# A new seed list for the list-scheduled order of a window-attention and mixer kernel

## The chip, the cores and the metric

The kernel runs on one core of one Trainium2 chip. The metric is device time in microseconds (us) from launch to end. The kernel before takes 262.97 us, the median of three runs (262.75 to 263.44). One further execution was recorded by the hardware profiler. Its span from the first to the last instruction is 261.5 us, and every time below that is not called a run time is taken from that record.

## The reference

Attention with four sink tokens and a window of 128 runs on (batch, heads, sequence, head size) = (4, 8, 768, 64). Its output, with the heads side by side as 512 columns, goes through a mixing layer along the sequence and a two-layer perceptron along the channels. All inputs and the output are float32.

```python
scores = q @ k.T / 8                       # per batch and head
keep   = (column < 4) | (0 <= row - column < 128)
a      = softmax(where(keep, scores, -1e9))
x      = a @ v                             # (4, 768, 512) with the heads side by side
a1     = alpha1 * x + beta1
u      = x + lam * (w_tok @ a1)            # w_tok is 768 x 768, over the sequence
a2     = alpha2 * u + beta2
out    = u + lam * (relu(a2 @ w_ch1) @ w_ch2)   # 512 -> 2048 -> 512
```

## The kernel before

The kernel does not issue its work in a written order. It first makes a list of tasks. A task is a short run of instructions on one engine (for example four matmuls, or one evacuation), with a priority, the engines that may do it and an expected duration on each in ns, the tasks that it needs, and the buffers that it uses.

```python
def add(self, prio, engs, fn, after=(), uses=(), mode=None, lands=None, port=False, since=0.0):
    t = Task(len(self.tasks), prio, engs, fn, after, uses, mode, lands, port, since)
```

A planner on the host then walks through time. Among the open tasks it takes the one that can start first by the expected durations; the rank, that is the order of the priorities, breaks ties. If a task has several engines it goes to the one where it would end first. The planner also gives out the buffers, so an order decides engines and buffers too. Two things are charged on TensorE: 95 ns whenever the packing of the array changes (`mode`), and a wait. Up to 36 us of planned time it fills waits of TensorE with matmuls on a constant tile ("idle" matmuls, whose result nobody reads).

```python
key = (at_e + FW * t.engs[e], at_e, r, at_e + t.engs[e], i, e)
# ... (cut: the choice of the best key over the open tasks)
n = int((start - max(free[PE], 400.0)) / (took if free[PE] > 4500.0 else 110.0))
if e == PE and free[PE] < until and n > 0:
    # ... (cut: takes a spare accumulator, if there is one)
    idle = (min(spare)[1], n)
# ... (cut)
if e == PE:
    if start < 4500.0:
        cost = cost * 2
    if t.mode != mode:
        cost = cost + 95
    mode = t.mode
free[e] = start + cost
if e == POOL or (e == DVE and t.port):
    port = free[e]
```

The last lines keep marked VectorE work and all GpSimd work from overlapping in the plan. Transfers go through a model of two queues (those that SyncE issues, those that GpSimd issues) that take turns.

The priorities are written by hand: loads at about -1000, the first attention batch below that or near -900, and the main work of batch b at 100*b and up. Then a list of seeds is applied, one after another. Each seed adds Gaussian noise to a random part of the priorities in one range.

```python
def shuffle(prio, seed):
    rnd = random.Random(seed)
    if seed < 100000:
        lo, hi, wide = -2200.0, 8.0, 10.0 ** rnd.uniform(0.7, 2.7)
    else:
        lo = rnd.choice((0.0, 0.0, 0.0, 50.0, 100.0, 200.0))
        hi, wide = lo + 60.0, 10.0 ** rnd.uniform(0.3, 1.3)
    share = 10.0 ** rnd.uniform(-2.5, -1.0)
    return [p + rnd.gauss(0.0, wide) if lo <= p < hi and rnd.random() < share else p for p in prio]

def emit(self, turns):
    prio = [t.prio for t in self.tasks]
    for seed in turns:
        prio = shuffle(prio, seed)
    for t, e, start, stop, idle in self.run(prio):
        # ... (cut: the instructions of the task are issued on engine e)
```

The tasks that the text speaks of are these. `mlp1` is the first matrix of the perceptron and its evacuation, `mlp2` the second, `tok` the mixing along the sequence, and `cast_w2` folds lam into the second matrix.

```python
# mlp1: four 128x384 matmuls, then relu on ScalarE or VectorE
a = add(p, {PE: 4 * 161}, mm, [...uT, w1...], [ph, bu])
done["h", b, chk, fi] = add(p + 0.1, {ACT: 493, DVE: 556}, relu, [a], [ph, bh])
# mlp2: four 128x512 matmuls of an accumulation over sixteen; the residual is added at its end
a = add(p, {PE: 4 * 214}, mm, [...hT, w2...], [pc, bh])
# tok: six 128x512 matmuls
a = add(p, {PE: 215 * len(sis)}, mm(sis), after, [pt] + [hs[si] for si in sis])
# cast_w2: sixteen of these
add(p, {DVE: 700, POOL: 1270},
    lambda e: engine[e].tensor_mul(w2f[:, a, :], src.t[:, a % 2, :], lam_b), [...wst, lam...], [src], port=True)
# scores of one block of 128 keys: row-packed, two accumulators of their own ("S", two in all)
a = add(p, {PE: cost}, mm, qk + [done["bias"]], [o] + [u[3] for u in units] + more, mode="row")
```

All other TensorE results share four accumulators (`"d": 4`). Per later batch there are six score tasks (row-packed) and one sink task (column-packed).

Of the kernel before, what the change touches and what calls it, by code (L numbers as in the profile page):

```python
# [276 lines left out]
def kernel(  # L277
# [130 lines left out]

    PAIRS = 3

    TURNS = (13523, 134113, 50022, 128275, 136711, 187603, 125671, 100730, 14946, 163131, 178432, 158827, 183776, 137680, 153375, 26742)
    W1_SINCE = 20000.0

    V0 = (((0, 1), (2, 3), (4, 5)), ((0, 1, 2), (3, 4, 5)))
# [799 lines left out]

    plan.emit(TURNS)

# [34 lines left out]
```

The softmax here doesn't subtract the row's maximum and nothing guards it: scores larger than these inputs give would overflow.

## Time and profile before

| | before |
|---|---|
| run time, median of 3 | 262.97 us |
| span in the profile | 261.5 us |
| TensorE matmul, busy | 254.1 us (97%) |
| VectorE, ScalarE, GpSimd, busy | 158.0, 132.5, 78.2 us |
| idle matmuls, busy | 9.5 us, 106 of them |
| mean granted TensorE clock | 1.000 |

The page of a profile has a row of busy times per engine, a strip of 40 slices of the span with the busy share in tenths, the chain of work that ended last (followed back from the last instruction), and the costliest groups of instructions. In a group, the name before the arrow is what is written and the names after it are what is read; then come sizes, type and count, the busy time and the mean of one. PE is TensorE's matmul side, PEld its weight loads, DVE VectorE, ACT ScalarE, POOL GpSimd and SP SyncE, which issues most transfers. The trace can also be asked for a timeline of one engine, for a table of busy times by stretch, and for the waits, that is who kept whom idle. A line such as L1007 is a line of the kernel's file: L1007 is mlp1's matmul, L1013 and L1015 its evacuation on ScalarE and VectorE, L1063 and L1034 mlp2's matmuls, L927 tok, L713 the scores, L909 the folding of lam into the second matrix, L344 the idle matmuls.

### The profile page before, as it was taken

The page shows a single profiled execution, that of the slowest core. Times are in us where ns is not written, and L with a number is a line of the kernel's source. Part 1 is how long each engine was busy: PE and PEld are TensorE (multiplying, and loading weights), DVE is VectorE, ACT ScalarE, POOL GpSimd, SP SyncE. Part 2 cuts the span into 40 slices and gives each one's busy share as a digit, 9 for nine tenths or more (in the row PEclk, how much of TensorE's full clock was granted, in tenths as well). Part 3 has the DMA queues.
Part 4 walks back from the last instruction along what each step waited for, and adds up shares of the span by engine and source line. Part 5 has one row for each costly group of instructions (what it writes and reads, how often), then busy time and mean ns, then how long its engine had stood idle before and what let it go on. Part 6 is the DMA issues. An engine that isn't in the chain of part 4 may idle for free.

```text
span 261.5 us, 4992 instructions
## 1 busy us (share of the span) xinstructions
PE 254.1 (97%) x1974; PEld 141.5 (54%) x1974; DVE 158.0 (60%) x321; ACT 132.5 (51%) x219; POOL 78.2 (30%) x97
## 2 busy tenths in 40 slices
PE   7999998998999999999999999999999999999994
PEld 7755645664555545655555445556554445664452
DVE  5787988989989946268967434376695352000221
ACT  1699746766665123788930133788610226772000
POOL 7429703634652420244544024003123000000000
PEclk9999999999999999999999999999999999999999
DMA  7999999999706987999928989200012136000222
GB/s 208 197 225 327 205 294 387 386 294 240 125 3 172 227 136 181 200 224 224 172 68 135 212 210 211 53 0 3 0 43 81 40 120 83 0 0 3 81 80 80
DMA packets 85839, 38.76 MB, mean 148 GB/s; under 512 B 73508, under 2 KB 79916, under 8 KB 85816
## 3 DMA queue, kind: packets, MB, share of 16 engines
q1 hardware_dynamic: 82032, 35.14, 55.0%
q0 software_dynamic: 3744, 3.28, 7.9%
q8 instruction: 15, 0.25, 0.4%
q14 instruction: 8, 0.07, 0.1%
q10 hardware_dynamic: 40, 0.03, 0.0%
HBM read 29.91 MB, written 6.29 MB: 138 GB/s over the span
## 4 chain that ended last, share of the span: by engine, by line
PE 82%; DVE 6%; DMA 6%; POOL 3%; issue 1%; ACT 1%; SPq 0%; POOLq 0%
PE ch L1063 31%; PE h L1007 28%; PE tok L927 9%; DVE w2f L909 4%; DMA w1f<-in_moe_w_ch_dram 4%; PE pv L803 4%; PE S L713 3%; DMA wst_w<-in_moe_w_ch_dram 2%; PE ch L1034 1%; POOL n L491 1%; PE tp L608 1%; PE tp L605 1%; PE idle L344 1%; DVE hT L1015 1%; ACT uT L951 1%
## 5 line engine op out<-in xcount | busy, mean ns | idle before, releaser
L1007 PE MATMUL h<-uT,w1f 128*128 128x384 f16 x512 | 88.8, 326 | 2.2 <-DVE hT L1015 1.1
L1063 PE MATMUL ch<-w2f,hT 128*128 128x512 f16 x368 | 86.5, 379 | 0.0
L1007 PEld LDWEIGHTS <-w1f 128*128 128x128 f16 x512 | 48.6, 98 | 34.8 <-issue 4.3
L1013 ACT ACTIVATE hT<-h 128x384 f16<-128x384 f32 x100 | 48.8, 490 | 29.5 <-PE h L1007 28.9
L1063 PEld LDWEIGHTS <-hT 128*128 128x128 f16 x368 | 34.3, 98 | 38.0 <-issue 1.1
L845 POOL TENSOR_TENSOR xh<-x,la_b 128x512 f16<-128x512 f32 x18 | 24.3, 1353 | 57.6 <-DVE x L829 57.5
L733 ACT ACTIVATE E<-S 128x1024 f16<-128x1024 f32 (+1 forms) x39 | 37.5, 1001 | 7.3 <-PE S L713 4.7
L1074 DVE TENSOR_TENSOR x<-x,ch 128x512 f32<-128x512 f32 x23 | 15.8, 686 | 35.1 <-PE ch L1063 35.0
L927 PE MATMUL tok<-xh,wtokT 128*128 128x512 f16 x144 | 33.9, 379 | 0.0
L351 ACT CAST u<-x 128x512 f16<-128x512 f32 x18 | 11.1, 618 | 43.1 <-DVE x L934 43.0
L934 DVE TENSOR_TENSOR x<-x,tok 128x512 f32<-128x512 f32 x24 | 16.3, 685 | 19.3 <-PE tok L927 19.3
L927 PEld LDWEIGHTS <-wtokT 128*128 128x128 f16 x144 | 14.0, 98 | 16.5
L852 DVE SCALAR_TENSOR_TENSOR x<-lb_b,rsum,x 128x512 f32<-128x512 f32 x24 | 19.9, 849 | 2.8 <-POOL xh L845 2.6
L829 DVE TENSOR_TENSOR x<-pv,rec 128x256 f32<-128x256 f32 x48 | 20.4, 424 | 1.9 <-DVE rec L828 0.2
L1015 DVE TENSOR_SCALAR hT<-h 128x384 f16<-128x384 f32 x28 | 15.3, 553 | 7.7 <-PE h L1007 7.5
L742 DVE TENSOR_TENSOR E<-E,maskn 128x1024 f16<-128x1024 f16 x24 | 18.4, 795 | 1.8 <-ACT E L733 1.7
L353 POOL CAST vfs<-vnat 128x512 f16<-128x512 f32 x18 | 13.0, 729 | 17.4 <-DMA vnat<-in_v_dram 16.3
L803 PEld LDWEIGHTS <-E 128*128 128x128 f16 x328 | 14.4, 97 | 6.5 <-issue 2.4
L803 PE MATMUL pv<-vfs,E 128*128 128x65 f16 x328 | 17.3, 194 | 0.0
L353 POOL CAST n<-nat 128x768 f16<-128x768 f32 x14 | 12.6, 915 | 14.7 <-DMA nat<-in_k_dram 11.6
L353 POOL CAST u<-x 128x512 f16<-128x512 f32 x6 | 3.7, 621 | 37.8 <-DVE x L934 15.8
L953 DVE TENSOR_SCALAR uT<-uT,ab 128x384 f16<-128x384 f16 x18 | 6.4, 407 | 12.6 <-DMA uT<-u 12.6
(107 smaller groups left out, 218.0 us busy)
## 6 DMA issues: line engine op xcount, KB each, us to landing
out_dram<-x SPq DMA_DIRECT2D x23, 256.0 KB, 2.3
nat<-in_q_dram SPq DMA_DIRECT2D x13, 384.0 KB, 5.8
nat<-in_k_dram SPq DMA_DIRECT2D x13, 384.0 KB, 5.8
vnat<-in_v_dram SPq DMA_DIRECT2D x18, 256.0 KB, 4.6
wst_w<-in_moe_w_ch_dram SPq DMA_DIRECT2D x8, 512.0 KB, 7.3
wtn<-in_moe_w_tok_dram SPq DMA_DIRECT2D x6, 384.0 KB, 4.4
w1f<-in_moe_w_ch_dram POOLq DMA_DIRECT2D x4, 512.0 KB, 10.1
v<-in_v_dram SPq DMA_DIRECT2D x12, 128.0 KB, 5.9
```

The source lines that it names most:

```text
L353: engine[e].tensor_copy(o, i)
L733: nc.scalar.activation(eT.t, pS.t[:, :, 0 : n * w].rearrange("p e (i w) -> p e i w", i=n), AF.Exp, scale=scale)
L742: nc.vector.tensor_mul(ev, ev, m.to_broadcast(list(ev.shape)))
L803: nc.tensor.matmul(po.t[:, hl, :], eT.t[:, e_, off + i, c : c + P], vf[j][:, h, :], start=(r < 2 and n == 0), stop=(n == len(parts) - 1 an ...
L829: nc.vector.tensor_mul(bx.t[:, 4 * G : 4 * G + 4, :], po.t[:, :, 0:D], rec.t.to_broadcast([P, 4, D]))
L845: engine[e].tensor_mul(bh.t, bx.t.rearrange("p h d -> p (h d)"), la1_b)
L852: engine[e].scalar_tensor_tensor(out=xf, in0=lb1_b, scalar=rsum[:, r : r + 1], in1=xf, op0=ALU.mult, op1=ALU.add)
L927: nc.tensor.matmul(pt.t, wtokT[:, si, ti * P : (ti + 1) * P], hs[si].t, start=(si == 0), stop=(si == NR - 1))
L1007: nc.tensor.matmul(ph.t, w1f[:, c, fi * P : (fi + 1) * P], bu.t[:, c, chk * NTOK : (chk + 1) * NTOK], start=(c == 0), stop=(c == NC - 1))
L1013: nc.scalar.activation(bh.t[:, fi, :], ph.t, AF.Relu)
L1015: nc.vector.tensor_scalar_max(bh.t[:, fi, :], ph.t, 0.0)
L1063: nc.tensor.matmul(pc.t, bh.t[:, fi, nt * P : (nt + 1) * P], w2f[:, fi, :], start=(fi == 0), stop=(fi == NF - 1))
```

## The change

Only the list of seeds is replaced: 16 seeds become 51. No instruction is added or removed by hand, and no size, buffer count or expected duration changes. The old list was the outcome of a search that tries seeds and keeps those that help the plan. The new list comes from a longer search over the whole program that may also keep a seed that lengthens the plan a little, so that it can leave a local optimum. The purpose is a better order. The planner reacts to the order with its choices of engine, of buffer and of the number of idle matmuls, so those may change too.

```diff
-    TURNS = (13523, 134113, 50022, 128275, 136711, 187603, 125671, 100730, 14946, 163131, 178432, 158827, 183776, 137680, 153375, 26742)
+    TURNS = (58916, 51094, 164988, 65830, 186405, 183280, 192278, 160001, 176913, 175892, 164653, 178892, 188107, 153507, 192130, 172908, 99824, 189726, 150232, 137815, 195819, 82470, 194072, 21991, 151693, 153696, 416, 91697, 101099, 129663, 169112, 142158, 173756, 141985, 173754, 121021, 159256, 87578, 8213, 167097, 92448, 86502, 130268, 29559, 103092, 138910, 127973, 143653, 120452, 45327, 124786)
```

## The prediction

> **What bounds the kernel now.** I read the busy times first, then the table by stretch, because an average over the span hides where an engine is idle. The busy row of the page:
>
> ```profile
> PE 254.1 (97%) x1974; PEld 141.5 (54%) x1974; DVE 158.0 (60%) x321; ACT 132.5 (51%) x219; POOL 78.2 (30%) x97
> ```
>
> TensorE is the bound; no other engine is busy for over 60%. But 97% counts the idle matmuls as work, and what a new order can win is only what TensorE does not have to do. The table by stretch (length, busy time of each engine with its instructions, clock, DMA share, GB/s) tells where that lies:
>
> ```profile
> 0.00:8.00 8.00, 6.66 (x74) 6.28 (x75) 4.49 (x20) 1.45 (x2) 6.30 (x17) 1.00 0.81 200
> 8.00:30.00 22.00, 21.89 (x323) 13.11 (x320) 18.05 (x50) 20.66 (x33) 12.91 (x21) 1.00 1.16 247
> 30.00:36.00 6.00, 6.00 (x36) 2.94 (x34) 5.93 (x11) 2.05 (x4) 1.11 (x2) 1.00 1.25 209
> 36.00:65.00 29.00, 26.67 (x215) 16.50 (x214) 25.76 (x36) 20.22 (x37) 12.27 (x13) 1.00 1.05 334
> 65.00:250.00 185.00, 185.00 (x1286) 97.73 (x1285) 100.84 (x202) 88.08 (x145) 45.58 (x46) 1.00 0.50 107
> ```
>
> From 65 to 250 us TensorE is busy for 185.00 of 185.00 us. An order can win there only by changing fewer packings, not by filling holes. From 36 to 65 us it is idle for 29.00 - 26.67 = 2.33 us, and VectorE is busy for 25.76 of those 29 us: that is the one stage where another engine holds TensorE up. From 0 to 30 us it looks full, but the same table for the idle matmuls alone says how much of it is filler:
>
> ```profile
> 5.20:8.00 2.80, 2.01 (x28) 1.00 1.12 203
> 8.00:18.00 10.00, 3.17 (x39) 1.00 1.25 215
> 18.00:30.00 12.00, 0.39 (x4) 1.00 1.08 274
> ```
>
> So 39 + 4 = 43 fillers run after 8 us. None run after 30 us.
>
> The timeline of TensorE around the holes (start, duration, group, idle time before it and who ended it):
>
> ```profile
> 39.43 0.32 PE L1007 MATMUL h<-uT,w1f 128*128 128x384 f16 x1 [0.48 <-ACT uT L951]
> 39.94 0.71 PE L1007 MATMUL h<-uT,w1f 128*128 128x384 f16 x2 [0.19 <-DVE uT L953]
> 41.03 2.27 PE L1007 MATMUL h<-uT,w1f 128*128 128x384 f16 x13 [0.38 <-ACT uT L951]
> ...
> 63.15 2.11 PE L1007 MATMUL h<-uT,w1f 128*128 128x384 f16 x12 [1.05 <-DVE hT L1015]
> ```
>
> Three holes at 39 to 41 us wait for the affine evacuations that make the first perceptron input. The largest, 1.05 us, waits for a relu on VectorE. The chain of waits, cut to that place, names what that relu stood behind:
>
> ```profile
> 57.58 0.56 DVE hT L1015
> 58.13 3.48 DVE w2f L909 x3
> 61.61 1.01 DVE E L742
> 62.63 0.48 DVE hT L1015
> 63.11 0.04 issue
> 63.15 2.11 PE h L1007 x12
> ```
>
> Three foldings of the second matrix and one mask, 4.5 us of VectorE, were issued between two relus. Reordering can address exactly this.
>
> **What the Trainium skill says, and whether the trace agrees.** "TensorE: Matmul & The Clock Gate", section "Wait — 56ns, not 53.3ns?", gives the spacing of warm matmuls as N/2.4 GHz + 2.5 ns. For N = 384 that is 162.5 ns; the chain has four mlp1 matmuls in 0.65 us, 162.5 each, so the steady state runs at the spacing of its columns and holds no hidden stall. For N = 128 it is 56 ns; the chain has twelve fillers in 0.67 us, which is 56 each. The section "What's actually happening" of the same page says that TensorE's clock falls to half after an idle window of about 3.4 us. The longest hole after 8 us here is 1.05 us and the granted clock is 1.00 in every stretch: it agrees, and an order would have to open a far longer hole to lose the clock. "SBUF — State Buffer", section "Who interferes with whom", says that a VectorE instruction with two SBUF inputs contends with a GpSimd instruction that reads SBUF. The foldings are such: on VectorE their median is 683 ns and their longest 1752 ns, and GpSimd was casting beside the slow ones. It agrees with that, and means that an order's value depends also on what GpSimd does at that moment.
>
> **The change part by part.** Nothing is removed or added but fillers; the necessary matmuls, evacuations and bytes stay. What moves, I worked out from the seeds: a seed under 100000 disturbs the front (priorities -2200 to 8), any other one of the windows. Evaluating each seed's range and share by the shuffle's own formulas and summing the shares: front 14 seeds and 0.27 expected nudges per task (before 4 and 0.15); window at 0, 6 and 0.28 (3 and 0.18); at 50, 3 and 0.04 (0 and 0); at 100, 7 and 0.28 (3 and 0.09); at 200, 21 and 0.83 (6 and 0.31). So the new list works most on the third batch, where the trace has no hole. Many of those seeds must be walking without gain, as a search that tolerates small losses does.
>
> The terms, each with its upper limit:
>
> 1. **Fillers after 8 us.** 43 x 56 ns = 2.4 us. They lie on the path: each is time in which TensorE had no task ready. They go only if the first attention's loads, casts and exponentials come earlier, and ScalarE is busy for 20.66 of 22 us in that stretch. I expect a fifth: -0.5 us.
> 2. **Holes from 36 to 65 us.** 2.3 us, of which the holes shown make 0.48 + 0.19 + 0.38 + 1.05 = 2.1. The 1.05 us hole needs only another order of VectorE's queue. The others depend on the evacuations after tok. I expect two fifths: -0.9 us.
> 3. **Packing changes.** A row-packed score task of eight 256-column matmuls takes 0.54 us in the chain. Two heads run side by side, so its columns need 4 x (256/2.4 + 2.5) = 0.44 us, and 0.10 us is the change. I counted 70 changes in the matmul records, 40 of them after 50 us, where three batches with seven packed tasks each can have 42 at most. Two S accumulators hold one score task, so two can hardly stand together. Limit about 0.3 us, expected -0.1.
> 4. **The first 8 us and the tail.** The last matmul ends at 257.9 us of 261.5; the residual and the last transfer make the other 3.6 us. The smallest last task is already a half tile, and no seed window reaches the last batch's priorities above 260 (its perceptron stands at 300 and up). Expected 0.
> 5. **Loss against the plan.** The plan counts fixed durations, while the chip showed a folding between 675 and 1752 ns and transfers share one set of queues. A new order fitted to the plan loses a little of its gain: +0.4 us.
>
> Sum: -0.5 - 0.9 - 0.1 + 0.4 = -1.1 us, and 263.0 - 1.1 = 261.9 us. The limits of terms 1 to 3 add to 2.4 + 2.3 + 0.3 = 5.0 us, and 2% is 5.3 us.
>
> **The rivals.** *A wait that takes the place of the one removed.* VectorE's work in 36 to 65 us is 25.76 of 29 us. If the foldings leave the relus' way, they must be done later, before mlp2 first reads them (69.5 us in the timeline), or on GpSimd at 1275 ns and more, where they can block VectorE in turn. For it: VectorE is nearly full. Against it: GpSimd is busy for only 12.27 us there. Result: 262.5 to 263.5 us, no change. *The loads move and the front gets longer.* 14 seeds disturb the front, which holds the order of the first transfers, and the DMA share there is over 1 in three stretches. The first quarter of the first perceptron matrix takes 10.1 us from issue to landing, and its landing at 32.8 us releases the transfers of the second matrix in the chain. For it: the plan's model of two rings is the roughest part. Against it: the old order was found with the same model and filled TensorE well. Result: 264 to 267 us. *A real improvement of the front.* A longer search may have removed most fillers and holes, half to two thirds of 5.0 us: 259.6 to 260.5 us. For it: a search that may go downhill reaches orders that the old one could not. Against it: the 16 old seeds have already taken the cheap gains.
>
> **Range and chances.** I give the middle case (261 to 263.2) six tenths, the improved front two tenths, the longer front somewhat under two tenths. That makes a range of 260.1 to 264.0. Faster by over 2% needs a time under 257.7, which is beyond all three limits together: 0.03. Slower by over 2% needs over 268.2, a stall of 5 us that the old order does not have: 0.03.
>
> **What would show each step.** Term 1: fewer than 43 fillers after 8 us. Term 2: less than 2.3 us idle from 36 to 65 us, with the relu no longer behind three foldings. Term 3: packing changes near 70. Term 4: 3.6 us from the last matmul to the end. The stretch from 65 us on should stay without a hole. The prediction is wrong if the start of the unbroken stretch moves by more than about 2 us, if a hole opens after 65 us, or if ScalarE's first exponentials shift with the loads.

## The result, and the profile after

The changed kernel takes 266.61 us, the median of four runs (266.18 to 268.01). The kernel before, on the same chip, takes 262.94 us. The ratio is 1.0146 (95% interval 1.0104 to 1.0187): slower by about 3.7 us, and outside the predicted range of 260.1 to 264.0 us. The span grew by as much, from 261.5 to 265.2 us. The busy row of the page of the changed kernel:

```profile
PE 255.6 (96%) x1971; PEld 141.5 (53%) x1971; DVE 159.7 (60%) x313; ACT 130.1 (49%) x221; POOL 84.8 (32%) x103
```

TensorE's work is nearly what it was, so the loss is idle time. What grew is GpSimd, from 78.2 to 84.8 us with six instructions more. Among its groups the casts of q and k rose from 14 to 17, and ScalarE's fell from 10 to 7. The table by stretch of the changed kernel (length, busy time and count of TensorE, its weight loads, VectorE, ScalarE and GpSimd, then clock, DMA share, GB/s):

```profile
0.00:8.00 8.00, 6.87 (x82) 6.70 (x82) 3.74 (x18) 2.67 (x3) 7.14 (x20) 1.00 0.74 163
8.00:30.00 22.00, 20.65 (x286) 11.81 (x286) 16.13 (x43) 18.11 (x32) 12.21 (x18) 1.00 1.08 246
30.00:36.00 6.00, 5.52 (x47) 3.00 (x47) 5.85 (x14) 2.16 (x4) 2.91 (x5) 1.00 1.24 207
36.00:65.00 29.00, 28.20 (x220) 16.88 (x219) 26.15 (x34) 18.65 (x38) 14.16 (x15) 1.00 1.04 325
65.00:250.00 185.00, 182.67 (x1274) 96.47 (x1271) 104.98 (x203) 88.47 (x149) 48.37 (x48) 1.00 0.49 110
```

From 36 to 65 us the idle time fell from 2.33 to 0.80 us, as the search meant it to. But 185.00 - 182.67 = 2.33 us of idle time opened after 65 us, where there had been none, and 1.35 + 0.48 us from 8 to 36 us, where there had been 0.11. The same table for the idle matmuls alone:

```profile
5.20:8.00 2.80, 2.21 (x33) 1.00 1.03 147
8.00:18.00 10.00, 2.20 (x21) 1.00 1.11 192
18.00:30.00 12.00, 1.18 (x12) 1.00 1.05 290
```

So 33 fillers ran after 8 us instead of 43. That looks like progress, but only because idle time that no filler covers stands in their place. The timeline of TensorE in the changed kernel shows where the idle time lies and who ended it:

```profile
9.07 0.53 PE L605 MATMUL tp<-iden,n 128*64 128x128 f16 x12 [1.14 <-DMA n<-in_k_dram]
...
66.61 2.76 PE L1007 MATMUL h<-uT,w1f 128*128 128x384 f16 x16 [1.54 <-DVE hT L1015]
...
82.72 0.39 PE L803 MATMUL pv<-vfs,E 128*128 128x65 f16 x7 [0.53 <-DVE E L742]
```

The largest hole, 1.54 us before 66.61 us, is of the same kind as the 1.05 us hole before it, and larger: a relu on VectorE behind foldings and a mask. The chain of waits of the changed kernel, cut to that place:

```profile
59.79 0.96 DVE qkT L353
60.75 4.33 DVE w2f L909 x4
65.08 1.01 DVE E L742
66.09 0.48 DVE hT L1015
66.57 0.04 issue
66.61 2.76 PE h L1007 x16
```

Four foldings take 4.33 us here. In the kernel's own plan the same four stand at 57.26 to 60.06 us and take 2.8 us. The same mask and the same relu follow them there too, but TensorE then waits only 0.04 us.

**Plan against chip.** The planner is part of the kernel, so its planned times can be set beside the record. For the end of the last matmul, with the two seed lists of this case and three orders from the experiments, each from one recorded execution:

| order | seeds | planned | on the chip | lag |
|---|---|---|---|---|
| hand-written priorities only | 0 | 258.11 us | 260.90 us | 2.8 us |
| before | 16 | 254.16 us | 257.90 us | 3.7 us |
| after | 51 | 253.37 us | 261.66 us | 8.3 us |
| mended plan, searched on from the old list | 35 | 254.80 us | 257.37 us | 2.6 us |
| mended plan, searched from the hand priorities | 66 | 254.86 us | 259.48 us | 4.6 us |

The longer search won 0.79 us in its plan and lost 3.76 us on the chip. The question for the experiments is what in the plan did not hold.

**Where the loss arises.** Orders differ, so equal times are not equal progress. I compare the time at which each kernel has done the same amount of necessary matmul work: its columns at the spacing that the prediction used, fillers left out, two heads side by side counted once. The table gives that time minus the time of the kernel before, in us, each from one profiled execution; the last column is the end of the last matmul.

| kernel, and what it is | at 24.1 | 30.5 | 45.5 | 61.1 | 67.7 | 88.3 | end |
|---|---|---|---|---|---|---|---|
| after | +1.28 | +2.13 | +1.54 | +1.67 | +1.88 | +3.47 | +3.76 |
| e5: old front, new rest | +0.82 | +1.18 | +0.24 | +0.09 | +0.28 | +1.86 | +2.15 |
| e6: new front, old rest | +0.76 | +2.44 | +2.46 | +2.14 | +1.96 | +1.97 | +1.97 |
| e7: after, late GpSimd casts on ScalarE | +1.04 | +1.89 | +0.62 | +0.41 | -0.98 | -0.13 | +0.38 |
| e11: e5 and e7 together | +0.95 | +1.30 | +0.78 | +0.64 | -0.75 | +0.10 | +0.63 |
| e12: before, one w_tok block later | +0.75 | +1.32 | +1.65 | +1.34 | +0.82 | +0.83 | +0.83 |
| e9: before, mended by hand | +0.74 | +0.85 | -0.42 | -0.56 | -1.58 | -1.58 | -1.58 |

The changed kernel loses in two places: up to 2.13 us by 30.5 us, in the front, and again between 61 and 88 us, where the second batch's attention runs.

Two limits of the table matter below. The recorded execution of the kernel before took 263.2 us, while the medians of its runs lie between 262.4 and 262.9 us, so at the end the table shows losses too small and gains too large by some tenths. And e5, e11 and e9 begin with the old order, yet stand at +0.74 to +0.95 at 24.1 us and at +0.85 to +1.30 at 30.5 us. In these three, and in e6 and e12, the buffers are given out anew after the edit. e8, which has the old order with its own buffers, stands at -0.01 and -0.02 by the same measure. Up to about a microsecond in the front of those five is therefore not due to what was moved, but to the buffers or to when transfers landed.

### The profile page after: what moved, and what is told of

Its sections match the earlier page's. It is cut to its first block, busy times and chain, and to the rows that moved or that the text cites. A ratio compares the mean times of both kernels' runs of the same rounds, so it can differ in the third digit from the quotient of the medians.

```text
span 265.2 us, 4985 instructions
## 1 busy us (share of the span) xinstructions
PE 255.6 (96%) x1971; PEld 141.5 (53%) x1971; DVE 159.7 (60%) x313; ACT 130.1 (49%) x221; POOL 84.8 (32%) x103
## 4 chain that ended last, share of the span: by engine, by line
PE 73%; DVE 15%; DMA 9%; POOL 1%; issue 1%; DVEq 0%
PE ch L1063 26%; PE h L1007 25%; PE tok L927 9%; DVE E L742 4%; DMA w1f<-in_moe_w_ch_dram 4%; DVE w2f L909 3%; PE pv L803 3%; PE S L713 2%; DMA la_b<-in_moe_alpha_dram 2%; DMA gates<-w1f 2%; DVE x L829 2%; DVE x L852 2%; PE ch L1034 1%; DVE hT L1015 1%; PE tp L608 1%; PE tp L605 1%
## 5 line engine op out<-in xcount | busy, mean ns | idle before, releaser
L1013 ACT ACTIVATE hT<-h 128x384 f16<-128x384 f32 x111 | 53.7, 490 | 36.4 <-PE h L1007 34.5
L845 POOL TENSOR_TENSOR xh<-x,la_b 128x512 f16<-128x512 f32 x18 | 25.3, 1408 | 52.9 <-DVE x L829 48.7
L351 ACT CAST u<-x 128x512 f16<-128x512 f32 x19 | 11.7, 617 | 36.8 <-DVE x L934 36.7
L852 DVE SCALAR_TENSOR_TENSOR x<-lb_b,rsum,x 128x512 f32<-128x512 f32 x24 | 22.4, 950 | 6.1 <-POOL xh L845 6.1
L353 POOL CAST n<-nat 128x768 f16<-128x768 f32 x17 | 16.2, 956 | 17.0 <-DMA nat<-in_k_dram 6.2
L742 DVE TENSOR_TENSOR E<-E,maskn 128x1024 f16<-128x1024 f16 x24 | 20.7, 881 | 0.2
L353 DVE COPY qkT<-tp 128x768 f16<-128x768 f16 x12 | 11.5, 957 | 3.4 <-PE tp L608 1.7
L1015 DVE TENSOR_SCALAR hT<-h 128x384 f16<-128x384 f32 x17 | 9.3, 553 | 5.9 <-PE h L1007 5.7
```

The costliest lines, as they stand in the source:

```text
L353: engine[e].tensor_copy(o, i)
L742: nc.vector.tensor_mul(ev, ev, m.to_broadcast(list(ev.shape)))
L845: engine[e].tensor_mul(bh.t, bx.t.rearrange("p h d -> p (h d)"), la1_b)
L852: engine[e].scalar_tensor_tensor(out=xf, in0=lb1_b, scalar=rsum[:, r : r + 1], in1=xf, op0=ALU.mult, op1=ALU.add)
L1013: nc.scalar.activation(bh.t[:, fi, :], ph.t, AF.Relu)
```

## The experiments

All kernels do the whole computation. All but three of them (e3, e13, e14) edit the list of planned steps after the planner has made it, just before the instructions are issued:

```python
steps = self.run(prio)          # the plan: (task, engine, start, stop, idle matmuls)
# the edit of an experiment stands here
for t, e, start, stop, idle in steps:
```

Ratios are to the kernel before on the same chip. The experiments ran on three chips (e1 to e8, e9 to e11, e12 to e14), so gains of different experiments are compared by their ratios.

**e1: the relu that TensorE waited for goes to ScalarE.** The new order is kept.

```diff
+ on = {288: ACT}          # the relu at 66.09 us; it was on VectorE
```

> The new order and its engines are kept instruction for instruction; only the one relu that stood behind four foldings and a mask on VectorE goes to ScalarE. In the new kernel TensorE was idle for 1.54 us before 66.6 us because of it. Theory A (VectorE falls behind its plan, because operations that the plan keeps apart on VectorE and GpSimd meet on the chip; the hole is where that lag is paid): the hole shrinks to under 0.3 us, and since VectorE stays late up to 90 us, part of the gain is given back there; 265.0 to 266.0 us against 266.6. Theory B (a plain misorder of one relu): the whole 1.5 us is won, 265.1 us. Theory C (the loss is made in the first 30 us and everything later is only its echo): the hole returns at the next relu, 266.3 us or more.

Measured: 266.02 us, ratio 1.0157 (1.0108 to 1.0206), so nothing was gained. The hole before 66.6 us was gone, but of the 1.6 us won there 0.85 was given back by about 70 us: VectorE was still behind, and TensorE's next task that needed it waited 0.67 us. In the recorded execution the clock also fell in the front (told at the end). This fits Theory A: the relu was a symptom.

**e2: the six casts of v for the second batch go from GpSimd to ScalarE.** Two of them, GpSimd's own folding and the start of a third cast ran beside the four foldings of VectorE. The timeline of GpSimd in the changed kernel:

```profile
62.13 0.73 POOL L353 CAST vfs<-vnat 128x512 f16<-128x512 f32 x1 [0.28 <-DMA vnat<-in_v_dram]
62.83 1.70 POOL L909 TENSOR_TENSOR w2f<-wst_w,lam_b 128x512 f16<-128x512 f32 x1
64.47 3.16 POOL L353 CAST vfs<-vnat 128x512 f16<-128x512 f32 x3
```

```diff
+ on = {i: ACT for i in range(341, 347)}
```

> The new order is kept; the six casts of v of the second batch go from GpSimd to ScalarE, 3.9 us of GpSimd work, which ran against VectorE's foldings and masks between 56 and 68 us. Theory A (meeting of VectorE and GpSimd): the four foldings that took 4.4 us take 2.4 to 3.5, the hole of 1.54 us before 66.6 us falls under 0.8, and the time to 265.0 to 266.0 us. Theory B (misorder of the relu alone): the foldings shorten or not, but the relu still stands behind them; the hole stays over 1.0 us and the time within 0.5 of 266.6. Rival: ScalarE, in order, waits for the loads of v in place of GpSimd and holds up the relus; over 267 us.

Measured: 265.62 us, ratio 1.0129 (1.0099 to 1.0160). The timeline of VectorE of this experiment (its file is three lines longer), the four foldings:

```profile
60.92 2.49 DVE L912 TENSOR_TENSOR w2f<-wst_w,lam_b 128x512 f16<-128x512 f32 x4
```

The same four instructions in the same queue take 2.49 us instead of 4.41 (the timeline's figure in the changed kernel), and the hole before the relu is gone. The Trainium skill, "SBUF — State Buffer", section "Who interferes with whom", says that a VectorE instruction with two SBUF inputs contends with a GpSimd instruction that reads SBUF. The trace agrees, and this gives the size: 1.9 us for four. It is not the size of the casts alone. GpSimd's own folding no longer stood behind a cast in its queue, and it too left the four:

```profile
58.89 1.27 POOL L912 TENSOR_TENSOR w2f<-wst_w,lam_b 128x512 f16<-128x512 f32 x1 [2.52 <-DMA wst_w<-in_moe_w_ch_dram]
```

The plan knows of the contention and keeps the two engines apart: it has the foldings from 57.26 us on and the next cast of v at 62.69 us, when it expects the load. On the chip the foldings began 3.4 us later than planned (60.66 us), and that cast 1.5 us earlier (61.23 us), as soon as its load had landed. So a late VectorE and a load that was quicker than planned met. The last matmul ended 1.1 us earlier than in the changed kernel, at 260.54 us, although the clock fell in this execution too.

**e3: no seeds at all.**

```diff
- TURNS = (13523, 134113, 50022, ...)
+ TURNS = ()
```

> The list of seeds is empty: the hand-written priorities alone. The plan gives its last matmul an end of 258.1 us, against 254.2 with the old seeds and 253.4 with the new. On the chip the last matmul ended 3.7 us after its plan with the old seeds and 8.3 us after it with the new. Theory S (the old list was picked among plans by its time on the chip, so its plan holds better than that of an order that was not): the empty list is late by 7 to 10 us like the new one, and the run takes 270 to 273 us. Theory N (the new list in particular has found what the plan gets wrong, and the lag of 3.7 us is the usual one): 266 to 268 us.

Measured: 266.41 us, ratio 1.0153 (1.0122 to 1.0184). The hand-written priorities, which the plan holds to be 4.7 us worse than the new list, are as fast as the new list. So the 51 seeds of the new list bought nothing on the chip that the hand order did not have, whereas the 16 old ones bought 4.0 us by the run times (3.0 us at the last matmul of the recorded executions). The hand order's lag of 2.8 us also speaks against Theory S: a lag of 7 to 10 us is not usual for an order.

**e4: the first block of w_tok is loaded, cast and transposed first, in the new order.** In the kernel before that block is done in dead time. Its VectorE timeline:

```profile
4.24 0.95 DVE L894 TENSOR_SCALAR_CACHE_REDUCE wt<-wtn 128x768 f16<-128x768 f32 x1 [0.64 <-DMA wtn<-in_moe_w_tok_dram]
...
6.12 0.56 DVE L353 COPY wtokT<-wT 128x768 f16<-128x768 f16 x1 [0.92 <-PE wT L887]
```

The new order begins its blocks of w_tok only here, while the first attention waits for VectorE:

```profile
24.14 0.94 DVE L894 TENSOR_SCALAR_CACHE_REDUCE wt<-wtn 128x768 f16<-128x768 f32 x1
25.56 0.94 DVE L894 TENSOR_SCALAR_CACHE_REDUCE wt<-wtn 128x768 f16<-128x768 f32 x1
```

```diff
+ first = the tasks 0, 27, 75, 76, 77 (load, cast, transposes, evacuation), ahead of all others
+ steps = first + rest
```

> The new order is kept, but the first block of the sequence matrix is again loaded first of all, cast, transposed and evacuated before the first queries and keys, as the old order had it; it takes 0.95 us of VectorE, six transposes and an evacuation of 0.56 us out of the busy stretch from 22 to 30 us. In the new kernel the same number of matmul columns is done 1.3 to 1.8 us later at 25 us than in the old. Theory F (the order of the first loads costs this): 265.0 to 265.8 us. Theory C' (the loss at the front is the transfers landing 1.2 us after their plan, whatever stands first): the first queries and keys land another 1 us later and nothing is won, 266.3 to 267.5 us.

Measured: 267.18 us, ratio 1.0188 (1.016 to 1.0216). Putting it first did harm: the load of the first k landed at 8.29 us instead of 5.34, because it now stood behind the block of w_tok, and the front was late by over a microsecond at once. In that order the block saved later did not pay that back. The time and the later k are as Theory C' has them, but C' also blames transfers that land late whatever stands first, and the first GpSimd transfer landed at 8.59 us here, against 9.03 us in the changed kernel. So that part is not shown. e12 asks the same question from the other side.

**e5 and e6: the two halves exchanged.** e5 takes from the old plan what starts before 29.9 us and the rest from the new one; e6 the reverse. The buffers are given out anew in the resulting order.

```diff
+ head = [s for s in old if s[2] < 29900.0]                       # e6: new
+ steps = head + [s for s in new if s[0].i not in begun]          # e6: old
```

> A splice of the two plans: everything that the old plan starts before 29.9 us, in the old order, then all the rest in the order of the new plan. In the profiles the new kernel has done the same matmul work 1.4 us later than the old at 25 us, 1.6 us later at 45, 2.2 us at 75, 3.5 us at 90 and 3.8 us at the end. Theory A (two causes that add: about 1.5 us of the loss arises in the first 30 us from transfers that land 1.2 us after their plan, about 2 us from 55 to 95 us where VectorE and GpSimd meet): 264.5 to 265.5 us. Theory C (the front alone; all later is its echo): 262.5 to 263.3. Theory D (the later part alone; a late front is swallowed by the waits after it): 266 to 267.

> The opposite splice: what the new plan starts before 29.9 us, in the new order, then the rest in the order of the old plan. Theory A: 263.8 to 264.8 us (the 1.5 us of the front alone). Theory C: 266 to 267. Theory D: 262.3 to 263.2. A splice may make a wait of its own at the seam; then both splices lie above what the theories say.

Measured: e5 265.53 us, ratio 1.0116 (1.0069 to 1.0163); e6 265.19 us, ratio 1.0119 (1.0084 to 1.0154). Each half alone is slower than the kernel before. In the table above e5 keeps the loss after 61 us and ends at +2.15, e6 keeps the loss in the front and ends at +1.97; together 4.1 us, where the changed kernel lost 3.76. The table by stretch, 65 to 95 us, first of e5 and then of e6:

```profile
65.00:95.00 30.00, 29.34 (x238) 15.41 (x238) 27.60 (x50) 13.17 (x17) 12.62 (x10) 1.00 0.62 129
```

```profile
65.00:95.00 30.00, 29.89 (x245) 15.94 (x245) 26.47 (x53) 14.13 (x18) 12.23 (x10) 1.00 0.63 140
```

With the new rest VectorE is busy for 27.60 of 30 us and TensorE has holes; with the old rest it is nearly full. By the run times the halves cost 3.0 and 3.1 us, more than the whole change when added. Each splice has a seam that neither search made, and buffers given out anew; of e6's +2.44 some 1.2 us arose between 30 and 31 us, at the seam. So only the place of each loss is read from here, not its size. That the front itself loses is seen better in kernels that keep its buffers: the changed kernel and e7 with the new front stand at +2.13 and +1.89 us at 30.5 us, e8 with the old one at -0.02.

**e7: in the new order every cast of q, k and v that the plan has on GpSimd after 55.5 us goes to ScalarE.**

```diff
+ on = {t.i: ACT for t, e, start, *_ in steps
+       if e == POOL and start > 55500.0 and kind(t) in ("trans", "cast_v")}
```

> The new order, with every cast of q, k and v that GpSimd starts after 55.5 us in the plan moved to ScalarE in its place. With the six casts of v alone moved, the hole before 66.6 us went and the last matmul ended 1.1 us earlier. Theory A (meeting of the two engines also makes the 1.2 us between 75 and 90 us): VectorE's operations with two inputs in SBUF are stretched by less still, the last matmul ends another 0.3 to 0.9 us earlier, 264.6 to 265.3 us. Rival (from 75 to 90 us VectorE is kept up by GpSimd's products for the next batch, which stay, or is simply too full): same as with six casts, 265.6 us. Rival 2 (ScalarE, in order, waits for loads): over 266.

Measured: 263.97 us, ratio 1.0070 (1.0048 to 1.0092), so about half of the loss is regained by the ratios (2.0 of 3.8 us), and more than Theory A had expected, with nothing in the order moved. The costliest groups of VectorE with two SBUF inputs, first in the changed kernel (count, then busy time and mean ns of one):

```profile
L852 DVE SCALAR_TENSOR_TENSOR x<-lb_b,rsum,x 128x512 f32<-128x512 f32 x24 | 22.4, 950 | 6.1 <-POOL xh L845 6.1
L742 DVE TENSOR_TENSOR E<-E,maskn 128x1024 f16<-128x1024 f16 x24 | 20.7, 881 | 0.2
...
L909 DVE TENSOR_TENSOR w2f<-wst_w,lam_b 128x512 f16<-128x512 f32 x12 | 11.9, 1036 | 0.0
```

and then in e7, whose file is four lines longer:

```profile
L856 DVE SCALAR_TENSOR_TENSOR x<-lb_b,rsum,x 128x512 f32<-128x512 f32 x24 | 20.0, 848 | 6.2 <-POOL xh L849 6.2
L746 DVE TENSOR_TENSOR E<-E,maskn 128x1024 f16<-128x1024 f16 x24 | 19.8, 837 | 0.9 <-ACT E L737 0.6
...
L913 DVE TENSOR_TENSOR w2f<-wst_w,lam_b 128x512 f16<-128x512 f32 x12 | 8.3, 734 | 0.0
```

The means fall from 950, 881 and 1036 to 848, 837 and 734 ns at equal counts. Taking for each group its tenth percentile as the undisturbed duration, the time above it summed over the three groups is 9.8 us before, 14.9 in the changed kernel and 7.2 in e7. For the whole of ScalarE the same measure gives 0.7 us before, 0.6 in the changed kernel and 2.7 in e7, where ScalarE does 28 casts more: it gives up 2 us for the 7.7 that VectorE wins.

A rival is that GpSimd, relieved of casts, serves others sooner. The rows show no sign of it: the wait of VectorE for GpSimd's products (`xh`) is 6.1 us before the edit and 6.2 after. A control is missing: all these casts on ScalarE in the old order. With six casts the gain is 0.4 us by the ratios in the new order (e2) and 0.3 us in the old one (e8 below), which the runs do not tell apart. That the casts hurt the new order more than the old rests on the recorded executions, 14.9 against 9.8 us.

**e8: the same six casts as in e2 to ScalarE, in the old order.**

> The old order, with the six casts of v of the second batch on ScalarE in place of GpSimd. The old kernel has a hole of 1.05 us before 63.2 us, behind three foldings that take 3.5 us beside GpSimd's casts. Theory A: the hole goes and the time falls by 0.6 to 1.1 us, to 261.3 to 261.8 on this chip. Theory B (order only; the casts do not matter): no change. If ScalarE waits for the loads of v in its order, it is slower by up to 2 us.

Measured: 262.09 us, ratio 0.9988 (0.9970 to 1.0007): no difference that is clear of noise, and less than Theory A's 0.6 us. In the recorded execution the three foldings took 2.32 us instead of 3.56 (the timelines' figures), the hole of the kernel before at 63 us was gone and the last matmul ended 1.35 us earlier. About 0.9 us of that is chance: the recorded execution of the kernel before took 0.7 us more than the median of its runs on this chip, and that of e8 0.3 us less than its own.

**e9: e8, and the last tok group moved behind the transposes that feed the first half of the perceptron.** On TensorE these transposes of u then come before the last tok group, so that ScalarE and VectorE can begin the affine evacuations for which the three holes at 39 to 41 us had waited. The buffers are given out anew.

```diff
+ on = {i: ACT for i in range(341, 347)}
+ moved = [s for s in steps if s[0].i == 229]      # the last tok group of the first batch
+ steps[k + 1:k + 1] = moved                       # k: the transposes of u, task 223
```

> The old order with two edits: the six casts of v of the second batch on ScalarE (as before, which alone gave a ratio of 0.9988), and the two transposes that feed the first perceptron half placed before the last matmul group of the mixing, not after it. In the old kernel TensorE was idle for 0.48 + 0.19 + 0.06 + 0.38 = 1.1 us at 39 to 41 us, waiting for the evacuations behind those transposes, and for 1.05 us at 63 us. If holes of TensorE before 65 us are what an order can win, both go and the time falls by 1.0 to 1.6 us against the old kernel, ratio 0.994 to 0.996. Rival: the mixing's last group now ends 0.7 us later, and its sum, cast and transposes hold up the second half; ratio 0.998 to 1.000.

Measured: 261.61 us over 22 runs, ratio 0.9967 (0.9952 to 0.9981), a gain of 0.9 us, just short of the forecast. In the recorded execution all four holes are gone. It beats both kernels: two hand edits, each aimed at holes seen in a profile, gained on the chip what 51 searched seeds did not.

**e10: in the new order the foldings of lam into the alpha and beta rows go later.** In the changed kernel VectorE waits 3.58 us for the first of these rows, at the head of its queue. Its timeline:

```profile
9.57 0.69 DVE L1113 TENSOR_TENSOR la_b<-la_b,lam_r 128x512 f32<-128x512 f32 x1 [3.58 <-DMA la_b<-in_moe_alpha_dram]
```

The plan started it at 7.99 us.

```diff
+ tasks 39, 40 behind 44; tasks 41, 42 behind 62
```

> The new order; on VectorE the folding of alpha into lam, which stood waiting 3.6 us for its row to land at 9.6 us, goes behind the masks and the first evacuations, the other one behind the last evacuation of the first batch's q and k. Theory E (the wait at the head of VectorE's queue makes the late front): 265.0 to 265.6 us. Theory F' (the pace of the front is that of GpSimd's transfers, the first of which landed at 8.2 to 9.3 us in every order so far, 9.0 here, where the plan has 7.75): masks come earlier, nothing else; 266.2 to 266.8.

Measured: 265.63 us over nine runs (263.93 to 267.39, and one of 271.01 us), ratio 1.0116 (1.0085 to 1.0147). For its question it is inconclusive: the first transfer that GpSimd issues landed at 8.40 us in the recorded execution and at 9.03 in the changed kernel, which alone moves the front.

That execution (264.06 us, the second fastest of the nine) shows something else. The casts and the foldings were not edited, but VectorE reached the four foldings 2.1 us earlier, and v landed 0.7 us earlier. VectorE and then GpSimd:

```profile
58.56 2.49 DVE L915 TENSOR_TENSOR w2f<-wst_w,lam_b 128x512 f16<-128x512 f32 x4
```

```profile
60.49 2.04 POOL L359 CAST vfs<-vnat 128x512 f16<-128x512 f32 x2 [5.34 <-DMA vnat<-in_v_dram]
```

The four take 2.49 us, as in e2, though every cast is still on GpSimd: they were nearly done when it began. The next three, which now ran beside GpSimd, took 3.79 us, against 2.30 in the changed kernel. So it is the meeting in time that stretches the foldings, and a shift of a microsecond or two decides which of them meet.

**e11: the old front of e5, with buffers given out anew, and the casts of e7.**

> Both suspected causes taken away at once: what the old plan starts before 29.9 us in the old order, then the new order, with the casts of q, k and v after 55.5 us on ScalarE. With the old front alone the profile's last matmul ended 2.15 us after the old kernel's, with the casts alone 0.4 us after it, with neither 3.8. Theory A (two causes that add): 2.15 - 3.4 = -1.2 us, so 261.3 to 262.3 us, at or below the old kernel. Rival (the casts' gain and the front's are the same slack counted twice): no better than the casts alone, 263.5 to 264.3.

Measured: 263.74 us over 20 runs, ratio 1.0027 (1.0010 to 1.0043). By the ratios about four fifths of the loss is regained, 1.1 us more than by the casts alone (e7). But the time lies in the rival's range, in the table it is no better than e7 from 68 us on, and Theory A's sum of both repairs is not reached. Some 0.7 us remains that neither explains.

**e12: the old order with the first block of w_tok moved to where the new order has it, 22 to 28 us.**

```diff
+ for i, behind in ((27, 26), (75, 123), (76, 73), (77, 74)):
+     steps: task i behind task `behind`
+ the buffers are given out anew
```

> The old order with one block moved: the first load of the sequence matrix goes behind the loads of v, its cast, transposes and evacuation from 4.2 to 6.7 us into the stretch from 22 to 28 us, as the new order has them. Theory G (that block, 0.95 + 0.08 + 0.56 us of VectorE in the busy stretch, is what makes the new front late): the same matmul work is 1.0 to 1.8 us later at 30 us than in the old kernel, 263.3 to 264.5 us. Rival (the queries and keys now land 1 us earlier and pay for it): within 0.4 us of the old kernel.

Measured: 264.49 us over five runs, ratio 1.0079 (1.0048 to 1.0110): by the run times the edited order is 2.1 us slower. How much of this the block makes is open. No run has the old order with buffers given out anew and nothing moved, and at 30.5 us the table has e12 (+1.32) hardly later than e11 with the old front (+1.30). ScalarE is idle for 3.0 us from 8 to 30 us, against 1.3 before and 3.9 in the changed kernel, but half of the increase lies before 12 us, while VectorE casts this block of w_tok only at 24 us. So that cast is at most a part of it. The recorded execution is the fastest of the five (263.99 us) and ends only 0.83 us late.

**e13 and e14: the plan mended, and searched again.** The time of a GpSimd transfer in the plan's queue model goes up to what the records show, the alpha and beta rows land at 9.6 us, and the casts that collided may no longer go to GpSimd. Nothing else in the planner changes. e13 continues from the old list (35 seeds), e14 starts from the hand priorities (66 seeds).

```diff
- WIRE = {"hw": 1600.0, "sw": 2100.0}
+ WIRE = {"hw": 1600.0, "sw": 3300.0}
- since=ROWS                          # 7000, the folding of the alpha and beta rows
+ since=9600.0
- cast of v: {POOL: 645}              # and {POOL, ACT} for q and k of the third batch on
+ cast of v: {ACT: 645}               # and {ACT} alone
```

> The plan is mended in three places that the profiles showed wrong, and searched anew from the old list: GpSimd's transfers land 1.2 us later in it, the folding of alpha can start at 9.6 us and not at 7, and the casts of v (and of q and k from the third batch on) may no longer go to GpSimd. In its own count the mended plan ends its last matmul at 254.8 us. Theory P (the chip's loss is what the plan gets wrong, and the new list had found just that): the order found holds with a lag of 3 to 4.5 us like that of the old list (3.7), not 8; 261.5 to 263.5 us, ratio 0.995 to 1.003. Theory Q (any long search on any plan drifts to orders that break): 265 us or more.

> The same mended plan, searched from the hand-written priorities and accepting losses on the way, 66 seeds, last matmul at 254.9 us in its own count. Theory P: 261.5 to 264 us. Theory Q: 265 us or more. If e13 holds and this one breaks, it was the old list that held, and not the mended plan.

Measured: e13 262.65 us over 22 runs, ratio 1.0001 (0.9987 to 1.0014); e14 264.36 us, ratio 1.0056 (1.0035 to 1.0077). e13 is as Theory P has it, but no faster than the old list from which it started. e14 lies between the two theories' ranges. As the table of lags shows, the fresh search lags by 4.6 us under the mended plan, against 8.3 for the longer search under the old one. The search of e14 is mine and not the one that made the new list, so the two lags are not strictly comparable, and the three mends are not told apart. That a more truthful plan lets a search go less astray is a reading that fits, not one that is shown.

## Why the prediction was wrong

**Term 5, the loss against the plan, is the step that failed.** It was put at +0.4 us. The lag went from 3.7 to 8.3 us, a loss of some 4.5. The reasons named in it were the right ones, varying foldings and shared queues, but I took them as noise around the plan, and sized them as if they were no worse in the new order than in the old.

One part of what stands in its place is shown. In the plan GpSimd's reads stay clear of VectorE's two-input instructions, and on the chip they do not: e2 and e10 take them apart in two different ways, and both times the four foldings fall from 4.41 to 2.49 us. Moving 28 casts (e7) regains 2.0 of the 3.8 us by the ratios.

The other part, the front, is shown only as to its place. The changed kernel is 2.1 us behind at 30.5 us, and the new front makes the old order slower (e6), but the splice has costs of its own. The first block of w_tok is a candidate that e12 does not settle. So is the first GpSimd transfer: it landed 1.3 us after its plan in the changed kernel (9.03 us against 7.75), and 0.4 us after it in the kernel before (8.67 against 8.30).

Why a longer search should end there is argued, not shown: among many orders it keeps those that look best on the plan, and these may be the ones that use most of what the plan gets wrong. The lags of 2.8, 3.7 and 8.3 us fit this, but they are three orders with one execution each. The prediction read the foldings of 675 to 1752 ns and the share of DMA over 1, and did not ask what a search makes of them.

**Terms 1 and 2** had the right direction, and their gain was lost elsewhere. Fillers fell from 43 to 33, and the idle time from 36 to 65 us by 1.53 us, more than the 0.9 expected. Both came back as idle time elsewhere: 1.7 us more from 8 to 36 us, 2.33 us after 65 us. The plan itself had won only 0.79 us, less than the 1.5 us that terms 1 to 3 add up to, so even a chip that followed the plan would have given somewhat less than predicted. Term 2 also read the 1.05 us hole as a matter of VectorE's order alone. e8 closes it with the order kept: the three foldings before it had taken 3.56 us beside GpSimd's casts, and take 2.32 us without them.

**Terms 3 and 4** held. The packing changes hardly moved: by the plan's own modes I count 78 in the record of the changed kernel and 76 in that of the kernel before (the prediction counted 70). And it is 3.5 us from the last matmul to the end, against 3.6. The sentence that the stretch from 65 us on should stay without a hole failed; it was, with the start of the unbroken stretch, one of the signs named for a wrong prediction. The slack there was smaller than the row of 185.00 us suggested: a full TensorE says nothing of how nearly VectorE was late, and VectorE was busy for 25.61 of the 30 us from 65 to 95 us already before.

**The rivals.** The longer front was given 264 to 267 us and under two tenths; the time lies in that interval. What it says, a longer front, is one part of what happened; that it is the order of the loads which makes it longer is not shown. The wait that takes the place of the removed one is the other part: a relu behind foldings and a mask once more, 1.54 us instead of 1.05. It was sized at no loss, as though foldings cost the same wherever they stand.

A folding's price depends on what GpSimd does at that moment. The prediction wrote exactly this beside its citation, and then did not carry it into a term.

## What to carry to other kernels

An order that a search found on a plan is only as good as the plan. Here another 0.79 us of planned gain stood against a lag that varied between 2.6 and 8.3 us from order to order: compare planned and recorded end for two or three orders before trusting another microsecond. Where GpSimd's reads meet VectorE instructions that combine two SBUF operands, try the work on ScalarE, even if the plan is indifferent; it gained 2.0 us in the new order (e7) and nothing clear of noise in the old (e8, six casts). Small edits aimed at holes in the record (e9) paid here where the search did not.

## What of the hardware was not expected

The prediction said that only a far longer hole than 1.05 us would lose TensorE's clock. In e1's profiled execution a wait of 2.00 us, ended by the first GpSimd transfer, was followed by half clock some 1.7 us later. The timeline of TensorE there (e1's file is three lines longer), and then its table by stretch:

```profile
9.35 0.53 PE L608 MATMUL tp<-iden,n 128*64 128x128 f16 x12 [2.00 <-DMA n<-in_k_dram]
```

```profile
11.00:14.00 3.00, 3.00 (x33) 1.72 (x34) 2.43 (x6) 1.79 (x5) 0.61 (x1) 0.52 1.28 205
14.00:17.00 3.00, 3.00 (x22) 0.73 (x16) 0.41 (x2) 1.46 (x3) 0.15 (x1) 0.50 0.78 162
```

The clock, the third number from the end, is 0.52 and 0.50 of full speed. In e2 a wait of 1.77 us at the same place did the same; after 1.14 us in the changed kernel and 1.44 us in e7 it stayed at 1.00. The Trainium skill, "TensorE: Matmul & The Clock Gate", section "What's actually happening", gives an idle window of about 3.4 us. Here the clock fell after a shorter single wait. In e1 TensorE was then busy for only 0.66 and 0.64 us of the next two microseconds, and what the wait did alone is not told apart from this. Across the recorded executions the first GpSimd transfer landed between 8.23 and 9.31 us with the new front, after 9.0 in four of seven, and between 8.27 and 8.90 us with the old one. So the new front risks a clock drop besides the wait. The execution of e1 with the drop took 268.12 us, its other three runs, at full clock, 265.2 to 266.46 us. The run of e10 that took 271.01 us had a mean clock of 0.981, the other eight 0.998 or more. This is why the front of e1 and e2 is not compared with others here.
